# Weights on a second load queue, single first tiles and a new step list in a fused windowed-attention and MLP kernel

## The chip, the cores and the metric

The kernel runs on one core of a Trainium2 chip. The metric is the device time of one execution in microseconds (us); the median of three runs is given, and one execution was also recorded by the profiler. The core has five engines with queues of their own: PE (TensorE, matrix multiplication, with its weight loads shown as PEld), DVE (VectorE), ACT (ScalarE), POOL (GpSimd) and SP (SyncE, which here only issues transfers). DMA transfers are issued from SP's, ACT's and POOL's queues and carried out by 16 DMA engines.

## The reference

Input x is 2048 rows of 512 (bf16). All weights are bf16.

```python
xn = layernorm(x)
# A: attention over 8 keys at distances 0, 2, ... 14; 32 heads of 16
q, k, v = split(xn @ wqkv)
logits = einsum(q, k[s - 2*w]) * 16 ** -0.5      # w = 0..7, masked where s - 2*w < 0
s = (softmax(logits) @ v[s - 2*w]) @ wo
# B: a mixer and an MLP
h = gelu(layernorm(xn) @ w1)                     # 512 columns in four groups of 128
hs = concat(h0 shifted by -1, h1 by +1, h2 by -2, h3 by +2 rows) @ w2
x1 = xn + hs
g = silu(x1 + gelu(layernorm(x1) @ w3) @ w4)     # 512 -> 1376 -> 512
out = x + s * g
```

## The kernel before

The 2048 rows are cut into 4 chunks of 512, and each chunk into 4 tiles: tile i holds every fourth row of its chunk, so that 16 tiles of 128 x 512 result. Every piece of work is a small Python function, a *step*. The string `ORDER` at the top lists all steps with their arguments, `name.arg.arg`, and a loop at the end calls them in that order (lines 14 to 70 and the loop behind `so`). Each engine works off its own instructions strictly in the order in which the list has issued them; waits between engines are inserted from the data. So the list is the schedule. Nothing else decides an order.

The steps that the change and the prediction speak of, with their lines in the kernel before:

- Loads. `ldxc` (L211) loads a whole chunk of x, 512 KB; `ldxp` (L221) a pair of tiles, 256 KB; `ldv` (L234) half of v's weights, `ldw1` (L241) half of w1, each 256 KB; `ldqk` (L228) the q half or the k half of the q and k weights, 512 KB; `ldw2` (L245) 512 KB, `ldw3`, `ldw4` and `ldwo` (L270, a quarter of wo) later weights. The letter after the name is the queue: s for SP, a for ACT, g for POOL.
- Constants. `c_warm` zeroes the operand of the warm-up matmuls; `c_zero` (L288 to L290) zeroes the 14 rows ahead of v in its DRAM scratch `v_dram` by a DMA from POOL's queue, and the halo columns of `hT` by two memsets; `c_elog` (L294 to L302) and `c_sel` (L310) build selection matrices on POOL; `sqw` (L315) makes ACT load its table early; `warmup.n.w.b` (L321) runs n matmuls of width w on zeros.
- The first chunk. `st` (L333) takes the row statistics of a tile on DVE, `sq0` (L338) the root on ACT, `nm0` (L344, L345) normalises on DVE, `tr0` (L356) transposes on PE, and `ev0h` or `ev0a` (L364, L360) brings the result to `xnT` on ACT. In later chunks `nmv` (DVE, L410) or `nm` (ACT, L417) normalises, with `rp`, `rs` (POOL, L386), `rr` and `nb` for the factors, and `xT.k` (L424) transposes a pair of tiles by a DMA on SP's queue.
- Products from `xnT`. `qk.c.n` (L443, four matmuls for one eighth of q and k of a chunk; `eqk`, L452, evacuates), `v.i` (L471; `ev` L481, and `sv`, L489, stores to `v_dram` from POOL's queue), `w1.i` (L496; `eh`, L507, with Gelu; `hTr`, L515, transposes on SP's queue).
- Attention. `pw` (L530) multiplies q with shifted k on DVE, `lg` (L543) sums over a head on PE, `smx`, `ex`, `sms`, `smn` are the softmax, `tE` (L598) transposes the weights, `vl` (L710) loads v's windows, `vp` (L716) weights them on DVE, `ws` (L729) sums on PE, `eo` (L743) evacuates, `oTr` (L748) or `oTp` with `eoT` (L756, L762) transposes, `wo` (L768) and `woh` (L793, half a tile) project.
- Mixer and MLP. `w2` (L611), `xa` (L618), `st3s`, `rq`, `r3`, `nm3` (L645), `x1Tr` (L655), `w3.c.f` (L668, 44 groups of four), `eg` (L677), `w4` (L685, 16 groups of eleven), `ya` (L692), `si` (L696).
- The end. `sg` (L775), or `ge` with `gb` (L782, L786), or `sgh` (L802) multiply s with g. For tiles 0 to 11 `pre` (L828) copies x into the output beforehand and `soa` (L835) adds on the way out; for tiles 12 to 15 `fav` or `favh` adds x on DVE and `so` or `soh` (L839, L813) stores.

The PSUM holds six accumulation banks, given as the last argument of a PE step, beside the two that `lg` uses.

Of the kernel before, what the change touches and what calls it, by code (L numbers as in the profile page):

```python
# [28 lines left out]
qk.1.6.3 xa.1 nb.7 qk.1.0.2 nb.6 st3s.1 eqk.1.6 hTr.3 rr.4 xa.0 ldw3.s.0 st3s.0 eqk.1.5 pw.0.6
nm.13 nm.12 nm.15 qk.1.7.0 qk.1.3.4 w2.2.5 w1.9.3 w1.8.1 eh.9 eh.8 xa.2 rr.7 hTr.4 rr.5 rq.0  # L30
w1.10.5 pw.0.7 r3.0 v.8.3 eh.10 st3s.2 nm.14 w2.3.1 nm3.0 nm3.1 eqk.1.3 w2.5.5 ev.8 qk.2.0.4
xa.3 st3s.3 eqk.1.7 eqk.1.0 xT.6 lg.0.3 rq.1 kh.2 xa.5 lg.0.2 r3.1 w2.4.2 smx.0 ldw3.s.1 sv.8
xT.7 x1Tr.0 v.10.5 qk.2.4.0 w2.6.1 eqk.2.4 nm3.3 xa.4 ex.0 w2.7.3 w1.11.2 xa.6 st3s.6 nm3.2 xa.7
qk.2.5.1 eqk.2.0 x1Tr.1 eh.11 ev.10 sv.10 rr.6 v.9.0 v.11.3 w1.13.4 eqk.2.5 ev.9 hTr.5 qk.2.7.2
w1.15.1 eqk.2.7 w1.12.0 vl.s.2.0 vl.s.0.0 ldw4.s.2 qk.2.2.2 vl.s.3.1 eh.12 pw.1.0 st3s.4 st3s.7
st3s.5 v.12.5 eqk.2.2 pw.1.3 sms.0 eh.13 v.13.0 w3.0.6.4 ev.11 hTr.6 rq.2 qk.2.1.3 pw.1.2 r3.2
sv.9 eg.0.6 eqk.2.1 ldwo.s.3 smn.0 rq.3 pw.1.1 r3.3 w3.0.1.2 qk.2.3.4 w3.0.10.3 nm3.4 eqk.2.3
tE.0 eh.15 eg.0.10 ev.13 eg.0.1 lg.1.1 lg.1.0 pw.1.7 w2.8.1 w1.14.0 w3.0.0.2 eh.14 w3.0.2.3
hTr.7 qk.2.6.0 eqk.2.6 eg.0.0 w2.10.4 nm3.6 vl.s.0.1 nm3.7 x1Tr.3 vl.s.1.0 pw.1.5 xa.8 pw.1.4
nm3.5 pw.1.6 w2.11.1 xa.10 w3.0.8.2 xa.11 qk.3.1.4 st3s.11 eg.0.8 ev.12 w2.14.1 lg.1.2 st3s.10  # L40
sv.12 lg.1.3 eqk.3.1 w2.12.4 sv.11 st3s.8 eg.0.2 smx.1 w2.9.3 ldw4.s.1 x1Tr.2 xa.9 w2.15.5 xa.14
w3.0.3.2 w3.0.9.3 xa.12 pw.2.2 qk.3.2.1 qk.3.0.4 w2.13.0 st3s.9 eqk.3.2 eqk.3.0 eg.0.3 vl.s.9.1
ldw4.s.0 rq.4 xa.15 vl.s.9.0 vl.s.3.0 ldwo.s.2 pre.s.2 qk.3.3.1 w3.0.5.2 st3s.12 qk.3.4.5 eg.0.5
pw.2.3 eqk.3.3 qk.3.5.4 st3s.14 pw.2.4 xa.13 pw.2.1 rq.5 st3s.15 v.15.1 eqk.3.5 v.14.2 ev.15
eqk.3.4 w3.1.1.0 w3.0.4.5 vp.0 st3s.13 rq.6 pw.2.0 r3.4 nm3.9 w3.0.7.1 eg.0.4 ev.14 eg.0.9
eg.0.7 ex.1 qk.3.7.4 w3.1.0.2 eg.1.0 sv.14 r3.5 nm3.10 rq.7 nm3.11 x1Tr.5 w3.1.8.1 vl.s.2.1
pre.s.1 vl.s.10.0 vl.s.10.1 w4.1.3 eqk.3.7 ldwo.s.1 kh.3 sv.15 r3.7 c_sel sms.1 w4.0.5 w4.2.4
ya.0 smn.1 r3.6 w3.1.5.5 w4.3.2 nm3.8 ya.2 ya.1 vp.1 x1Tr.4 w3.1.9.3 nm3.15 eg.1.5 ya.3 w3.1.6.4
pre.s.0 vp.3 tE.1 w3.1.7.2 eg.1.6 eg.1.1 w3.1.3.5 w3.1.4.0 eg.1.7 vp.2 lg.2.1 lg.2.0 qk.3.6.2
eg.1.8 w3.1.10.1 eqk.3.6 nm3.14 pw.2.5 pw.2.7 w3.1.2.4 eg.1.3 eg.1.10 eg.1.4 lg.2.2 pw.2.6  # L50
x1Tr.7 eg.1.2 ws.2.1 ws.1.0 ws.0.4 eg.1.9 pw.3.2 ws.3.3 eo.1 lg.2.3 eo.0 smx.2 vl.s.4.1 w4.6.0
w3.2.0.4 oTr.0 eo.2 eo.3 oTr.1 vl.s.5.1 pw.3.0 ex.2 vl.s.4.0 vl.s.6.0 vl.s.5.0 w4.5.3 vl.s.6.1
ya.6 pw.3.4 w4.7.0 w4.4.1 w3.2.3.5 sms.2 si.2 si.1 si.3 eg.2.0 eg.2.3 si.6 vl.s.7.1 vl.s.7.0
pw.3.1 pw.3.5 nm3.12 ya.4 wo.1.4 nm3.13 ya.7 w3.2.2.1 sg.1 w3.2.9.0 vp.4 ya.5 w3.2.5.4 w3.2.4.5
eg.2.9 w3.2.1.2 smn.2 x1Tr.6 w3.2.8.0 vp.5 eg.2.4 eg.2.2 eg.2.5 w3.2.10.1 w3.2.7.4 w3.2.6.5
eg.2.7 eg.2.10 eg.2.1 eg.2.8 vp.6 tE.2 vl.s.8.1 vl.s.8.0 wo.0.3 eg.2.6 wo.2.1 wo.3.0 pw.3.3 sg.2
w4.10.5 soa.2 sv.13 sg.3 vp.7 w3.3.0.0 lg.3.0 eg.3.0 lg.3.2 si.4 pw.3.6 pw.3.7 ws.4.0 ws.5.1
lg.3.1 ws.7.2 ws.6.4 eo.4 ya.10 lg.3.3 vl.s.11.1 w4.9.0 smx.3 eo.5 si.7 si.0 eo.7 si.5 eo.6
si.10 vl.s.13.1 oTr.2 vl.s.13.0 vl.s.11.0 w4.8.2 vp.9 vl.s.12.1 ex.3 oTr.3 w4.11.4 ya.8 ya.9
sms.3 ya.11 smn.3 w3.3.7.0 w3.3.5.2 w3.3.1.5 eg.3.5 vp.10 tE.3 wo.4.4 eg.3.7 eg.3.1 vl.s.14.1  # L60
vl.s.12.0 sg.0 vl.s.14.0 vp.11 w3.3.4.1 w3.3.9.2 w3.3.10.5 eg.3.10 w3.3.8.0 w3.3.3.3 w3.3.6.5
eg.3.9 eg.3.4 vp.8 w3.3.2.1 eg.3.6 eg.3.8 wo.6.2 eg.3.2 eg.3.3 wo.7.0 sg.6 vp.13 ws.10.3 ws.9.2
eo.10 ws.11.1 ws.8.5 eo.9 w4.13.3 vl.s.15.0 sg.4 vl.s.15.1 vp.12 eo.11 eo.8 wo.5.4 si.11 oTr.5
vp.14 si.9 w4.12.5 oTr.4 w4.15.1 ya.12 sg.5 si.12 si.8 sg.7 vp.15 w4.14.0 soa.1 soa.0 soa.3
# [810 lines left out]
```

## Time and profile before

| | us |
|---|---|
| runs | 189.74, 190.42, 190.26; median 190.26 |
| profiled execution, its own time | 190.75 |
| its span, first to last instruction | 189.0 |
| PE busy / PE weight loads | 182.8 (97%) / 87.0 |
| DVE busy | 165.1 (87%) |
| ACT busy | 112.8 (60%) |
| POOL busy | 42.7 (23%) |
| chain that ended last, share of PE | 85% |
| granted TensorE clock, mean | 0.996 |

The page names an instruction by the line of the program that issued it, its engine and operation, and the tiles that it writes and reads, `out<-in`. In rows of the chain of waits a piece has its start, its length and what it was; SPq is the time that SP took to issue a transfer. In a timeline a bracket at the end gives the idle time of the engine before the piece, and what ended it. A transfer's time to landing runs from the start of its issue to the moment at which all of its data have arrived.

### The profile page before, as it was taken

How to read it: one execution, taken by the hardware profiler on the slowest of the kernel's cores; microseconds unless marked ns; L12 is line 12 of the kernel's file. 1: busy time of each engine (PE TensorE's matmuls, PEld its weight loads, DVE VectorE, ACT ScalarE, POOL GpSimd, SP SyncE). 2: the span in 40 equal slices, each digit the busy share in tenths (PEclk: the TensorE clock that was granted, in tenths of full speed). 3: DMA queues.
4: the chain of work that ended last, by engine and by line, in shares of the span. 5: the costliest groups of instructions: out<-in, count | busy, mean ns of one | idle time of the engine just before them, and what ended most of it. 6: DMA issues, size and time to landing. Idle time of an engine off the chain costs nothing.

```text
span 189.0 us, 3685 instructions
## 1 busy us (share of the span) xinstructions
PE 182.8 (97%) x1430; PEld 87.0 (46%) x1430; DVE 165.1 (87%) x270; ACT 112.8 (60%) x189; POOL 42.7 (23%) x70
## 2 busy tenths in 40 slices
...
GB/s 164 315 352 115 199 248 141 194 238 137 233 120 286 278 64 224 222 87 190 399 162 361 274 57 134 254 401 277 189 190 95 254 335 238 210 254 106 88 106 116
DMA packets 47842, 39.25 MB, mean 208 GB/s; under 512 B 35251, under 2 KB 41889, under 8 KB 47777
## 3 DMA queue, kind: packets, MB, share of 16 engines
...
q0 software_dynamic: 2528, 3.69, 10.9%
...
q10 hardware_dynamic: 288, 0.20, 0.3%
...
## 4 chain that ended last, share of the span: by engine, by line
PE 85%; DMA 4%; DVE 4%; issue 2%; POOL 2%; SPq 1%; ACT 1%; POOLq 0%
PE mm L668 20%; PE mm L685 18%; PE mm L443 15%; PE mm L611 8%; PE mm L496 7%; PE mm L471 6%; PE lg L543 4%; PE mm L768 4%; DMA xc<-in_A_x_dram 3%; PE mm L729 3%; POOL out_dram L835 2%; DMA out_dram<-xr 1%; DVE st L333 1%; DVE xr L775 1%; DVE xr L786 1%
## 5 line engine op out<-in xcount | busy, mean ns | idle before, releaser
L530 DVE TENSOR_TENSOR pw<-qT,kT 128x2048 bf16<-128x2048 bf16 x32 | 38.3, 1214 | 3.4 <-PE lg L543 2.4
L668 PE MATMUL mm<-x1T,w_sb 128*128 128x512 bf16 (+1 forms) x176 | 40.9, 379 | 0.0
L685 PE MATMUL mm<-w_sb,h 128*128 128x512 bf16 (+1 forms) x176 | 39.4, 379 | 0.0
L677 ACT ACTIVATE h<-mm 128x512 bf16<-128x512 f32 (+1 forms) x44 | 23.9, 602 | 23.3 <-PE mm L668 17.6
L716 DVE TENSOR_TENSOR vs<-vs,att 128x4096 bf16<-128x4096 bf16 x16 | 36.2, 2285 | 0.0
L443 PE MATMUL mm<-xnT,wqk_sb 128*128 128x512 bf16 x128 | 30.6, 379 | 0.0
L835 POOL DMA_DIRECT2D out_dram<-xr x12 | 11.0, 1117 | 74.0 <-DVE xr L775 74.0
L668 PEld LDWEIGHTS <-w_sb 128*128 128x128 bf16 (+1 forms) x176 | 17.6, 100 | 20.4
L685 PEld LDWEIGHTS <-h 128*128 128x128 bf16 (+1 forms) x176 | 16.9, 98 | 20.8 <-issue 0.4
L443 PEld LDWEIGHTS <-wqk_sb 128*128 128x128 bf16 x128 | 12.4, 98 | 15.0
L452 ACT ACTIVATE kT<-mm 128x512 bf16<-128x512 f32 x16 | 9.4, 601 | 12.1 <-PE mm L443 11.9
L489 POOL DMA_DIRECT2D v_dram<-vt x16 | 9.6, 601 | 30.6 <-ACT vt L481 27.2
L471 PE MATMUL mm<-w2v_sb,xnT 128*128 128x512 bf16 x64 | 15.8, 379 | 0.0
L496 PE MATMUL mm<-w_sb,xnT 128*128 128x512 bf16 x64 | 15.8, 379 | 0.0
L611 PE MATMUL mm<-w2v_sb,hT 128*128 128x512 bf16 x64 | 15.7, 380 | 0.0
L768 PE MATMUL mm<-wo_sb,oT 128*128 128x512 bf16 x60 | 14.3, 379 | 0.0
L333 DVE BATCH_NORM_STATS2 st<-xc 128x6 f32<-128x512 bf16 x16 | 10.8, 676 | 3.9 <-DMA xc<-in_A_x_dram 3.9
L452 ACT ACTIVATE qT<-mm 128x512 bf16<-128x512 f32 x16 | 9.4, 605 | 7.8 <-PE mm L443 7.7
L635 POOL TENSOR_TENSOR rstd<-nmr,mhalf 128x2 f32<-128x2 f32 x8 | 9.1, 1136 | 19.8 <-DVE nmr L628 19.7
L507 ACT ACTIVATE ht<-mm,rs 128x512 bf16<-128x512 f32 x16 | 10.6, 690 | 4.4 <-PE mm L496 2.3
L696 ACT ACTIVATE xr<-xr 128x512 bf16<-128x512 bf16 x16 | 9.6, 630 | 6.0 <-DVE xr L692 6.0
L692 DVE TENSOR_TENSOR xr<-mm,xr 128x512 bf16<-128x512 f32 x16 | 10.6, 683 | 1.1 <-PE mm L685 0.9
...
## 6 DMA issues: line engine op xcount, KB each, us to landing
...
xc<-in_A_x_dram SPq DMA_DIRECT2D x4, 256.0 KB, 5.9
...
```

The lines of the kernel that those rows point to most:

```text
L443: nc.tensor.matmul(pt, lhsT=wqk_sb[:, dt, nt * P : (nt + 1) * P], rhs=xnT[c][:, :, dt, :], start=(dt == 0), stop=(dt == ND - 1),)
L452: nc.scalar.activation(dst.rearrange("p (n i) -> p n i", i=TPC), mm.pop(("qk", c, nt)).rearrange("p (i n) -> p n i", i=TPC), AF.Copy,)
L471: nc.tensor.matmul(pt, lhsT=xnT[c][:, jj, dt, :], rhs=wv_sb[:, dt, :], start=(dt == 0), stop=(dt == ND - 1),)
L496: nc.tensor.matmul(pt, lhsT=xnT[c][:, jj, dt, :], rhs=w1_sb[:, dt, :], start=(dt == 0), stop=(dt == ND - 1),)
L530: nc.vector.tensor_tensor(out=pw_t[c, u], in0=q_t[c], in1=k_t[c][:, :, DIL * u : DIL * u + CH], op=ALU.mult)
L611: nc.tensor.matmul(pt, lhsT=hT[:, plane, g, p0 : p0 + P], rhs=w2_sb[:, g, :], start=(g == 0), stop=(g == ND - 1),)
L668: nc.tensor.matmul(pt[:fs, :], lhsT=w3_sb[:, dt, ft * P : ft * P + fs], rhs=x1T[c][:, :, dt, :], start=(dt == 0), stop=(dt == ND - 1),)
L677: nc.scalar.activation(h3[c, ft][:fs, :], mm.pop(("w3", c, ft))[:fs, :], AF.Gelu_apprx_tanh)
L685: nc.tensor.matmul(pt, lhsT=h3[c, ft][:fs, jj * P : (jj + 1) * P], rhs=w4_sb[:fs, ft, :], start=(ft == 0), stop=(ft == NF - 1),)
L716: nc.vector.tensor_tensor(out=vv, in0=vv, in1=att[c][:, :, H * jj : H * jj + H].unsqueeze(2).to_broadcast([P, NB * 2, DH, H]), op=ALU.mult,)
L768: nc.tensor.matmul(pt, lhsT=oT[i // 2][:, i % 2, dt, :], rhs=wo_sb[:, dt, :], start=(dt == 0), stop=(dt == ND - 1),)
L835: nc.gpsimd.dma_start(out=rows(out2, i), in_=xr[i], accum_op=ALU.add)
```

## The change

Four things are changed. v's weight halves go out from ACT's queue, beside x on SP's. The first pair of x tiles is loaded by two transfers of one tile each (a new step `ldx`) where there was one of two tiles. The zeroing `c_zero` stands later in the list. And the whole list of steps is new: the same computing steps on the same engines, in another order and partly with other accumulation banks (five short warm-up matmuls stand where there were eight). The unused step `fag` is taken out and an unused step `preh` is put in.

The head of the list up to the first steps of chunk 1, and its end:

```diff
-ldxp.s.0 c_warm c_small warmup.10.512.0 sqw c_ident kh.0 ldv.s.0 ldv.s.1 ldxp.s.1 ldw1.s.0
-ldw1.s.1 c_zero st.0 ldxp.s.2 ldxp.s.3 st.1 sq0.0 ldqk.s.0 ldqk.s.1 nm0.0 sq0.1 rp.0 nm0.1
-tr0.0.0 warmup.8.128.1 ev0h.0.0 ev0h.0.1 st.2 tr0.1.2 v.0.1 st.3 ev0h.1.0 ev0h.1.1 sq0.2 v.1.2
-ev.0 nm0.2 sq0.3 rp.1 w1.0.0 ev.1 nm0.3 rs.0 sv.0 st.5 tr0.2.1 ldxc.s.2 w1.1.2 ev0a.2 sv.1 rr.0
-st.4 tr0.3.3 rs.1 v.2.1 ev0a.3 st.7 rp.2 rs.2 w1.2.4 ev.2 st.6 eh.0 v.3.3 sv.2 rp.3 rr.1 w1.3.1
-nmv.4 nmv.5 ev.3 qk.0.1.5 xT.2 eh.1 sv.3 qk.0.0.3 rs.3 qk.0.3.2 eh.2 eh.3 eqk.0.1 c_elog
-qk.0.4.1 qk.0.5.5 nmv.6 nmv.7 st.11 ldxc.s.3 st.10 st.8 eqk.0.3 eqk.0.5 qk.0.2.2 eqk.0.0
-qk.0.6.4 eqk.0.2 st.9 eqk.0.4 qk.0.7.3 eqk.0.6 eqk.0.7 pw.0.1 rp.5 st.15 st.13 rp.4 xT.3 hTr.0
-ldw2.s hTr.1 w1.4.1 v.5.4 ldwo.s.0 ev.5 w1.5.3 v.4.2 ev.4 qk.1.4.4 rs.4 sv.4 v.6.5 w1.7.2 rr.3
+ldx.s.0 ldx.s.1 c_warm kh.0 ldv.a.0 warmup.10.512.0 ldv.a.1 c_small c_ident sqw st.0 st.1 sq0.0
+nm0.0 sq0.1 nm0.1 rp.0 c_elog ldxp.s.1 ldw1.s.0 ldw1.s.1 ldxp.s.2 ldqk.s.0 ldxp.s.3 st.2 st.3
+ldqk.s.1 tr0.0.1 warmup.5.128.0 ev0h.0.0 ev0h.0.1 tr0.1.2 v.0.0 ev0h.1.0 ev0h.1.1 sq0.2 v.1.1
+ev.0 sq0.3 ev.1 rs.0 nm0.2 w1.0.2 nm0.3 tr0.2.0 tr0.3.1 w1.1.3 ev0a.2 v.2.0 ldxc.s.2 ldwo.s.3
+rr.0 rp.1 sv.0 sv.1 rs.1 ev0a.3 qk.0.0.1 w1.2.4 eqk.0.0 ev.2 qk.0.3.5 st.5 st.4 rp.2 st.6 rs.2
+st.7 nmv.4 rp.3 eh.1 nmv.5 sv.2 rr.1 qk.0.4.0 st.8 xT.2 rs.3 st.9 qk.0.1.1 c_sel eh.0 nmv.6
+qk.0.7.3 eh.2 eqk.0.1 eqk.0.4 nmv.7 rp.4 ldxc.s.3 st.10 qk.0.5.2 rs.4 xT.3 st.11 qk.0.2.1
+eqk.0.5 eqk.0.7 rp.5 qk.0.6.0 hTr.0 rr.4 eqk.0.2 rs.5 eqk.0.3 v.3.3 eqk.0.6 w1.3.5 ev.3 pw.0.3
+v.4.0 eh.3 sv.3 w1.5.3 hTr.1 rr.2 ev.4 w1.4.5 sv.4 nb.4 ldw2.s c_zero qk.1.3.0 st.14 eqk.1.3
+rr.3 st.15 st.13 eh.5 qk.1.6.1 eqk.1.6 pw.0.1 st.12 nm.9 w1.7.2 eh.4 rp.7 rp.6 rs.6 qk.1.7.3
+ldw4.s.2 hTr.2 nb.5 pw.0.0 rr.5 qk.1.4.1 v.5.5 w1.6.0 eqk.1.7 eh.6 v.6.3 pw.0.2 nb.6 nm.8 rs.7
+rr.7 rr.6 w2.1.4 ev.5 ev.6 xT.4 nm.10 w2.0.0 v.7.5 vl.s.1.0 xa.0 nm.12 eqk.1.4 xa.1 lg.0.0
...
-soa.7 soa.5 soa.4 soa.6 ya.13 ya.15 si.13 ws.13.4 ya.14 ws.15.3 ws.12.1 ws.14.5 eo.15 wo.8.0
-si.14 eo.14 wo.9.3 sg.8 eo.12 eo.13 wo.10.1 soa.8 sg.9 si.15 oTp.13.4 soa.9 sg.10 oTp.14.3
-eoT.13 oTp.12.0 wo.11.5 eoT.12 oTp.15.4 eoT.14 wo.13.0 eoT.15 wo.14.3 wo.12.4 woh.15.0.1
-woh.15.1.2 soa.10 sg.11 soa.11 ge.13 gb.13 ge.14 fav.13 gb.14 so.s.13 ge.12 fav.14 gb.12 so.s.14
-sgh.15.0 fav.12 favh.15.0 so.a.12 sgh.15.1 soh.s.15.0 favh.15.1 soh.a.15.1
+sg.10 soa.7 soa.10 soa.1 ya.14 ya.13 si.14 ws.14.2 ws.13.3 ws.12.4 ya.12 ya.15 ws.15.1 wo.11.0
+eo.14 si.13 eo.13 si.11 eo.15 wo.9.3 sg.11 eo.12 oTp.14.1 soa.11 sg.9 wo.8.0 eoT.14 si.12 soa.9
+oTp.12.3 sg.8 oTp.13.1 eoT.12 wo.14.4 eoT.13 soa.8 oTp.15.3 ge.14 wo.12.0 eoT.15 gb.14 wo.13.4
+ge.12 fav.14 so.s.14 woh.15.0.3 gb.12 ge.13 woh.15.1.0 fav.12 si.15 gb.13 so.a.12 fav.13
+sgh.15.0 so.s.13 favh.15.0 sgh.15.1 soh.s.15.0 favh.15.1 soh.a.15.1
```

The steps:

```diff
     @step
+    def ldx(q, i):
+        if 0 not in x_c:
+            x_c[0] = rot("xc", 0, 2, [P, TPC, D])
+        qs[q].dma_start(out=xtile(i), in_=rows(x2, i))
+
+    @step
     def ldxc(q, c):
...
-    @step
-    def fag(i):
-        nc.gpsimd.tensor_tensor(out=xr[i], in0=xtile(i), in1=xr[i], op=ALU.add)
-
...
+    @step
+    def preh(q):
+
+        def half(t):
+            return t[(NCH - 1) * CH :, :].rearrange("(p i) d -> p (i d)", i=TPC)[:, 0 : 2 * D]
+
+        qs[q].dma_start(out=half(out2), in_=half(x2))
```

More of the change, by code (lines that the diff above doesn't have):

```diff
@@ L23 @@
-qk.0.4.1 qk.0.5.5 nmv.6 nmv.7 st.11 ldxc.s.3 st.10 st.8 eqk.0.3 eqk.0.5 qk.0.2.2 eqk.0.0
-qk.0.6.4 eqk.0.2 st.9 eqk.0.4 qk.0.7.3 eqk.0.6 eqk.0.7 pw.0.1 rp.5 st.15 st.13 rp.4 xT.3 hTr.0
-ldw2.s hTr.1 w1.4.1 v.5.4 ldwo.s.0 ev.5 w1.5.3 v.4.2 ev.4 qk.1.4.4 rs.4 sv.4 v.6.5 w1.7.2 rr.3
-rr.2 eh.4 pw.0.2 kh.1 ev.6 sv.5 rs.5 nb.4 pw.0.0 st.12 eqk.1.4 eh.5 w1.6.1 qk.1.1.4 qk.1.2.3
-v.7.5 hTr.2 nm.8 nm.9 w2.1.0 pw.0.3 nb.5 rp.6 eh.6 xT.4 vl.s.1.1 eh.7 st.14 rp.7 lg.0.0 rs.7
-eqk.1.2 lg.0.1 ev.7 pw.0.5 w2.0.5 rs.6 eqk.1.1 nm.11 nm.10 pw.0.4 sv.7 qk.1.5.4 sv.6 xT.5
@@ L29 @@
[L29 to L64, printed above, removed]
@@ new lines @@
+eqk.0.5 eqk.0.7 rp.5 qk.0.6.0 hTr.0 rr.4 eqk.0.2 rs.5 eqk.0.3 v.3.3 eqk.0.6 w1.3.5 ev.3 pw.0.3
[3 more added lines that the diff above has]
+rr.7 rr.6 w2.1.4 ev.5 ev.6 xT.4 nm.10 w2.0.0 v.7.5 vl.s.1.0 xa.0 nm.12 eqk.1.4 xa.1 lg.0.0
+lg.0.1 eh.7 st3s.1 w2.3.4 qk.1.5.2 qk.1.1.1 nm.11 hTr.3 ev.7 nm.13 pw.0.4 xT.5 w2.2.5 eqk.1.5
@@ new lines @@
+sv.5 kh.1 sv.7 w1.8.2 st3s.0 pw.0.6 ldw3.s.0 eh.8 pw.0.7 v.8.0 xa.3 qk.1.2.3 nb.7 pw.0.5 nm.14
+qk.1.0.4 w1.9.2 eqk.1.1 xT.6 eqk.1.0 v.9.1 eh.9 st3s.3 rq.0 eqk.1.2 hTr.4 ev.8 lg.0.3 lg.0.2
+xa.2 st3s.2 rq.1 nm.15 w1.10.3 smx.0 xT.7 qk.2.7.0 eh.10 qk.2.6.2 w1.11.3 eqk.2.6 v.10.5 kh.2
+sv.6 r3.1 sv.8 r3.0 nm3.3 nm3.2 ev.9 x1Tr.1 sv.9 w2.5.1 ev.10 eh.11 v.11.2 xa.5 eqk.2.7 hTr.5
+nm3.1 pw.1.2 pw.1.3 nm3.0 w2.6.3 ev.11 w1.13.0 ldw3.s.1 w1.12.2 eh.13 x1Tr.0 eh.12 xa.6 st3s.5
+ex.0 v.12.1 ldw4.s.0 hTr.6 qk.2.3.0 w1.15.3 qk.2.2.2 w2.7.5 pw.1.0 pw.1.1 ev.12 w1.14.1 eh.15
@@ new lines @@
+st3s.6 w2.8.4 xa.7 eh.14 st3s.7 qk.2.0.3 vl.s.3.1 vl.s.1.1 hTr.7 v.14.1 w2.4.5 eqk.2.3 eqk.2.0
+sv.11 vl.s.0.0 ldw4.s.1 ldwo.s.0 eqk.2.2 lg.1.1 lg.1.0 vl.s.0.1 w3.0.6.2 sms.0 xa.4 rq.3 r3.3
+st3s.4 pw.1.5 w2.9.5 eg.0.6 w3.0.3.3 rq.2 xa.9 r3.2 sv.10 pw.1.6 w3.0.0.2 eg.0.3 ev.14 sv.14
+w2.10.5 qk.2.4.1 eqk.2.4 eg.0.0 nm3.4 nm3.6 nm3.7 pw.1.4 nm3.5 w2.11.3 qk.2.5.0 x1Tr.3 eqk.2.5
+xa.8 smn.0 x1Tr.2 qk.2.1.2 w3.0.8.4 eg.0.8 pw.1.7 w3.0.7.0 qk.3.5.1 eqk.2.1 vl.s.2.1 tE.0
+w3.0.2.2 eqk.3.5 w3.0.9.4 st3s.9 xa.11 st3s.11 st3s.8 eg.0.9 eg.0.2 lg.1.3 lg.1.2 vl.s.2.0
```

23 lines of the change are left out of this document (added).

## The prediction

> **What bounds the kernel now.** I read the page's busy table first (PE 182.8 of 189.0 us), then the chain of waits in order of time, then stretches with the busy time of each engine, and last the DMA view cut down to single issues.
>
> The stretches (us, then busy us and instructions of PE, PEld, DVE, ACT, POOL; clock; DMA share; GB/s):
>
> ```profile
> 16.00:170.00 154.00, 153.98 (x1255) 73.36 (x1254) 142.97 (x214) 94.38 (x155) 29.29 (x44) 1.00 0.90 216
> 170.00:184.60 14.60, 14.55 (x107) 7.07 (x104) 10.57 (x16) 8.85 (x16) 6.99 (x8) 1.00 0.76 102
> ```
>
> From 16 to 184.6 us PE idles for 0.07 us in all. Both step lists hold the same computing steps (three warm-up matmuls aside; fag and preh are in neither), so nothing can be gained there: the new list can only start this dense stretch earlier, end it faster, or tear holes into it. What holds its start back is the chain of the first 16 us (start, length, what):
>
> ```profile
> 0.73 0.40 SPq L221
> ...
> 2.15 5.68 DMA xc<-in_A_x_dram
> ...
> 7.85 0.71 DVE st L333
> ...
> 9.64 0.42 DVE xr L345
> ...
> 10.11 0.40 PE mm L356 x4
> 10.51 0.94 PE mm L496 x4
> ```
>
> The second pair of x tiles (I call it p1) is issued at 2.15, behind x0 and both halves of v's weights on SP's queue, and lands at 7.83; statistics and normalisation take 2.28 us more, and tr0.2 starts at 10.11. PE in that time:
>
> ```profile
> 5.87 0.61 PE L356 MATMUL mm<-ident,xr 128*128 128x128 bf16 x4 [0.24 <-DVE xr L345]
> ...
> 7.06 1.94 PE L471 MATMUL mm<-w2v_sb,xnT 128*128 128x512 bf16 x8
> 8.83 1.03 PE L496 MATMUL mm<-w_sb,xnT 128*128 128x512 bf16 x4
> 10.11 0.40 PE L356 MATMUL mm<-ident,xr 128*128 128x128 bf16 x4 [0.26 <-DVE xr L345]
> ```
>
> A group of four matmuls costs 0.8635 us where PE is dense (32 of qk in 6.91). v.0, v.1 and w1.0 (2.59) run from 7.06 to about 9.70, then PE waits. The DMA view, one issue each in order of issue (KB, us from issue to landing):
>
> ```profile
> xc<-in_A_x_dram SPq DMA_DIRECT2D x1, 256.0 KB, 2.9
> w2v_sb<-in_A_wqkv_dram SPq DMA_DIRECT2D x1, 256.0 KB, 3.1
> w2v_sb<-in_A_wqkv_dram SPq DMA_DIRECT2D x1, 256.0 KB, 5.5
> xc<-in_A_x_dram SPq DMA_DIRECT2D x1, 256.0 KB, 5.7
> w_sb<-in_B_w_dram SPq DMA_DIRECT2D x1, 256.0 KB, 5.8
> w_sb<-in_B_w_dram SPq DMA_DIRECT2D x1, 256.0 KB, 6.0
> ```
>
> Added to their issue times in SP's timeline (0.73, 1.18, 1.64, 2.15, 2.66, 3.14) this is a ladder: 0.25 MB in at 3.6, 0.50 at 4.3, 0.75 at 7.17, 1.0 at 7.83, 1.25 at 8.5, 1.5 at 9.18; the next rows go on with 2.0 at 10.5, 2.5 at 12.0, 3.0 at 13.3. v's second half lands 0.3 us before the third matmul of v.0 needs it. In 2 to 7 us the DMA share is 0.79, 0.88, 0.78, 0.74 and 0.83, so 0.98 us of engine time lie idle there.
>
> **The change, part by part.** *Start.* SP now issues x0 and x1 (128 KB each), p1, w1's halves, pair 2, q's half of wqk, pair 3, k's half. ACT issues v's halves at about 0.73 and 1.1.
> - p1 is issued at 0.73 + 2 × 0.45 = 1.6 instead of 2.15, with only 0.5 MB through its own ring. How the two rings share is not in this trace. Bounds: if v waits, p1 completes 0.50 MB (4.3); if v goes first, 1.0 MB (7.83). Middle 0.75 MB: 7.17.
> - v's second half completes 0.75 MB if v goes first (7.17), 1.5 MB if x and w1 go first (9.18). Middle 1.125 MB: 8.17.
> - Two rings can fill the idle 0.98 us; bounds 0 and 0.98. I take three quarters, 0.73, since the zeroing DMA of POOL (issued 1.50, 0.73 us) leaves this stretch too. So p1 at 6.4, v at 7.45, w1's second half at 8.45.
>
> x0 alone (half the bytes of the pair) should be in by about 3.0 to 3.6, and the ten warm-up matmuls end at 5.63 either way, so tr0.0 moves from 5.87 to 5.63 and v.0 from 7.06 to about 6.7 (five short warm-ups instead of eight, 0.08 each). Then: v.0's third matmul waits for 7.45; v.0 ends at 7.88, v.1 at 8.74, w1.0 at 9.61 (its third matmul needs w1 by 9.18). tr0.2 is ready at 6.4 + 2.28 = 8.7 and costs no wait; two transposes at 0.22 reach 10.05. Five groups (w1.1, v.2, w1.2, v.3, w1.3, in whatever order among qk) end in effect at 10.05 + 4.32 = 14.37. Before, that point was 15.13. **Gain 0.76 us.** At 7.17 it would be 1.04, at 8.17 only 0.04.
>
> By the Trainium skill, "DMA: Bandwidth & Descriptors", section "Issuing engines are not separate DMA queues", queues of different engines feed the same 16 DMA engines and a second issuer saves only issue time. By that rule v's second half comes earlier by 0.4 us of issue alone, 8.17 - 0.4 = 7.77, and the gain would be 0.44; the idle DMA share above speaks for some more.
>
> *ACT.* The two issues (0.37 each by ACT's rows at the end) push the table load (1.28) and the first Sqrt (0.20) from 2.22 to about 2.96; the first real Sqrt comes at 4.56 now and not before 3.8 then. Nothing, with 0.8 us of cover; beyond that it would cost its excess on x0's chain.
>
> *POOL.* The zeroing (DMA issue 0.73, two memsets of 0.35; it zeroes v_dram's pad rows and hT's halo) moves behind sv.4, where POOL idles 6.01 us in front of 25.89; its first readers on PE are w2.1 and w2.0 at about 31. The constants e_log (2.35 us, now at 17.52) go into POOL's idle time before 5.98. Both nothing.
>
> *SP.* ldwo.3 (0.74) now stands ahead of xT.2, and pair 3 behind q's half of wqk, so pair 3 lands at the 2.5 MB step, 12.0 - 0.7 = 11.3 instead of 10.5. DVE reaches st.6 at about 11.6, so it hides. q's half lands at the 2.25 MB step, 11.2; qk.0.0, now right after v.2, wants it at 10.05 + 1.73 = 11.78.
>
> *The list after 16 us.* I added up each engine's steps with spacings from the rows (pw 1.13, vp 2.20, xa, ya and sg 0.61, smx 2.4; lg 0.58, ws 0.46, w4 2.38 on PE). PE work ahead of the first ws of each chunk, minus DVE work up to that chunk's last vp: before 10.2, 9.2, 10.5, 10.9; after 10.6, 10.5, 10.2, 12.3. For the first w3 against the last nm3: before 12.2, 22.7, 23.7, 21.3; after 14.6, 21.2, 36.3, 30.5. The cover is no thinner, so I cost the reordering at nothing between 16 and 184 us. If that is wrong, each us that a producer is late costs a us, since PE has no idle time to absorb it.
>
> *Tail.* After the last ge (0.60) DVE still has gb, fav, two sgh and two favh before the last store, as now (184.34 to 186.29). si.15 (0.53) moves behind the last ge on ACT and is done 0.2 us before sgh.15.0. Nothing.
>
> **Sum.** The profiled execution took 190.75 (span 189.0 and 1.75 around it); it would become 189.99 with a span of 188.24. The median of the runs is 0.49 lower, 190.26: forecast **189.50**. The unknown terms alone give -1.1 (PE runs without a wait from 6.7: 6.7 + 2.59 + 0.44 + 4.32 = 14.05) to about 0: 189.1 to 190.3.
>
> **Rivals.** *A: hidden anyway.* The 16 groups between tr0.3 and qk.1.3 end at 10.05 + 13.82 = 23.87. qk.1.3 needs the transpose xT.3, now issued at 18.89 behind a 512 KB x load, 5.6 us to landing, at 24.49. If it lands no earlier than now, PE waits 0.62 and 0.14 of the gain is left: 190.1. For it: it hangs on pair 3, which comes later. Against: the wait of 2.45 us for POOL's rs that delays it now should shrink, and I get 17.5 for its issue.
>
> *B: the other side, v's weights late.* Place: the third matmul of v.0. If SP's ring, filled first and longer, is served ahead of ACT's, v's second half comes with 1.5 MB, at 9.18. Then v.0 ends at 9.61, w1.0 at 11.34, and the point at 15.13 becomes 16.10: 191.2. It decides from 8.2 on (no gain); each later us costs a us. For it: v.0 is only 0.3 us from waiting now. Against: ACT's issues are as early as SP's. The Trainium skill, "DMA: Bandwidth & Descriptors", section "Queues, rings and completion order", says that each DMA engine takes turns between its queue rows packet by packet; by that rule B would not happen. No run here shows two hardware rings at the start.
>
> *C: a hole later in the list.* w2's weights (4.2 us to landing now) are issued behind hTr.1, which needs w1.3, done at 10.05 + 13 × 0.8635 = 21.3 instead of 15.1. With the evacuation (0.69) and hTr.1's own issue (1.34) they go out at 23.4, and w2.1 wants them at 23.87 + 8 × 0.8635 = 30.8. At the slowest 512 KB row (8.2) they come at 31.6: 0.8 us. Two such holes make 0.76 - 1.6 a loss of 0.84: 191.1.
>
> **How the numbers follow.** Within 0.5% (0.95 us, about what a measurement of this kernel can tell from no change) means 189.31 to 191.21. Forecast 0.62, of which 0.28 lies below 189.31 (v by about 7.2) and 0.34 within. A 0.12, all within. B 0.15 and C 0.11, of which a wait somewhat past the price worked out, 0.24, goes beyond 191.21 and 0.02 stays within; the share beyond is large because a late transfer has no upper bound in these rows. Faster 0.28, same 0.48, slower 0.24. The forecast's own range is 189.1 to 190.2; with half of B and C outside and 0.3 for the spread of the runs the range is 188.8 to 191.4.
>
> **What would show it.** Right: p1 at 6.4 ± 0.5, v.0's third matmul at 7.2 to 7.8, the first of tr0.2 before 9.8, PE without idle time from there to about 183.8, zeroing at 23 to 26 on POOL with nobody waiting. Wrong: a PE gap at v.0 past 8.2 (B), at qk.1.3 (A), at w2.1 (C), or any PE idle time over 0.3 us between 16 and 184.

## The result, and the profile after

| | before | after |
|---|---|---|
| median of 22 runs | 189.88 (189.74 to 190.50) | 190.41 (190.26 to 192.31) |
| ratio, 95% interval | | 1.003 (1.0019 to 1.0041) |
| profiled execution / its span | 190.75 / 189.0 | 190.69 / 188.9 |

The changed kernel is 0.5 us slower, not 0.8 faster. The two profiled executions hide it, as they took the same time; that of before was 0.87 over its kernel's median. So a second one of before, from the first experiment (189.95, span 188.2, called "before again" below), is set beside that of after. The median of 22 runs of before is also 0.38 below that of the three runs from which the forecast was counted (190.26).

The stretches of after (start:end, length, busy us and instructions of PE, PEld, DVE, ACT, POOL; clock; DMA share; GB/s):

```profile
16.00:170.00 154.00, 153.06 (x1241) 73.31 (x1253) 141.08 (x211) 94.37 (x155) 24.87 (x38) 1.00 0.85 214
170.00:184.60 14.60, 14.23 (x104) 6.96 (x103) 10.60 (x17) 8.69 (x16) 7.37 (x9) 1.00 0.82 121
```

PE is nearly as dense as before. Of the 0.94 us of idle time up to 170, twelve are single steps of 0.05, 0.63 in all, which I put down to missing records of matmuls (14 fewer than in before's stretch); two are waits, of 0.16 and 0.15. The chain of after's start (start, length, what):

```profile
0.74 0.39 SPq L212
...
1.19 3.55 DMA xc<-in_A_x_dram
...
4.76 0.70 DVE st L339
...
5.67 0.06 DVE rs L350
...
5.75 0.42 DVE xr L351
...
6.22 0.40 PE mm L362 x4
```

The chain runs over the second single tile, x1: issued at 1.19, in at 4.74. VectorE has the statistics of x1 (L339) in front of the normalization of x0 (L350, L351), so x0, in at 3.65, helps nothing. The transfers of after, one issue each in order of issue (KB, us to landing; issued at 0.74, 0.74, 1.19, 1.25 and 1.65):

```profile
w2v_sb<-in_A_wqkv_dram ACTq DMA_DIRECT2D x1, 256.0 KB, 3.6
xc<-in_A_x_dram SPq DMA_DIRECT2D x1, 128.0 KB, 2.9
xc<-in_A_x_dram SPq DMA_DIRECT2D x1, 128.0 KB, 3.5
w2v_sb<-in_A_wqkv_dram ACTq DMA_DIRECT2D x1, 256.0 KB, 4.2
xc<-in_A_x_dram SPq DMA_DIRECT2D x1, 256.0 KB, 4.5
```

PE of after, at the start and at the one later wait that a rival had named:

```profile
6.22 0.40 PE L362 MATMUL mm<-ident,xr 128*128 128x128 bf16 x4 [0.59 <-DVE xr L351]
...
7.10 1.90 PE L477 MATMUL mm<-w2v_sb,xnT 128*128 128x512 bf16 x8
...
9.70 0.61 PE L362 MATMUL mm<-ident,xr 128*128 128x128 bf16 x8
...
24.28 1.04 PE L449 MATMUL mm<-xnT,wqk_sb 128*128 128x512 bf16 x4 [0.16 <-DMA xnT<-xr]
```

tr0.2 starts at 9.70 without a wait, as forecast. But before again has that too. Its chain, and the landing of its p1 (issued at 2.15):

```profile
0.73 2.63 DMA xc<-in_A_x_dram
...
5.78 0.50 PE mm L356 x4
...
9.58 0.22 PE mm L356 x4
...
14.34 6.91 PE mm L443 x32
```

```profile
xc<-in_A_x_dram SPq DMA_DIRECT2D x1, 256.0 KB, 4.1
```

Its x pair is in at 3.36, its first transposes start at 5.78, p1 is in at 6.20, and from 5.78 on PE has no idle time over 0.03. The last line is the point that the prediction puts at 15.13 in the profile of before and forecasts at 14.37:

```profile
15.13 6.91 PE mm L443 x32
```

Before again has it at 14.34 without any change. Of these 0.79 us, 0.42 are the wait for p1 (w1.0 to tr0.2 takes 10.11 - 8.83 there, 9.41 - 8.55 here), 0.28 a later v.0 (7.06 and 6.78), and 0.09 lie behind tr0.2. Between the first transposes and PE's last product the two kernels need the same (184.29 - 6.22 = 178.07 and 183.76 - 5.78 = 177.98). VectorE's last steps, before again first, then after:

```profile
183.55 0.43 DVE L786 TENSOR_TENSOR xr<-vt,xr 128x512 bf16<-128x512 bf16 x1
183.90 0.42 DVE L802 TENSOR_TENSOR xr<-mm,xr 128x256 bf16<-128x256 f32 x1
184.23 0.41 DVE L819 TENSOR_TENSOR xr<-xc,xr 128x512 bf16<-128x512 bf16 x1
...
185.22 0.29 DVE L807 TENSOR_TENSOR xr<-xc,xr 128x256 bf16<-128x256 bf16 x1
```

```profile
184.07 0.42 DVE L792 TENSOR_TENSOR xr<-vt,xr 128x512 bf16<-128x512 bf16 x1
184.53 0.43 DVE L825 TENSOR_TENSOR xr<-xc,xr 128x512 bf16<-128x512 bf16 x1
184.88 0.42 DVE L808 TENSOR_TENSOR xr<-mm,xr 128x256 bf16<-128x256 f32 x1
...
185.99 0.29 DVE L813 TENSOR_TENSOR xr<-xc,xr 128x256 bf16<-128x256 bf16 x1
```

VectorE ends 1.75 behind PE's last product before (185.51 - 183.76), 1.99 after (186.28 - 184.29). So 0.44 is lost at the first transposes, 0.09 in between and 0.24 at the end: 0.77, against 0.74 between the two executions' times.

### The profile page after: what moved, and what is told of

It is laid out like the page before. It is cut to its first block, busy times and chain, and to the rows that moved or that the text cites. A ratio compares the mean times of both kernels' runs of the same rounds, so it can differ in the third digit from the quotient of the medians.

```text
span 188.9 us, 3664 instructions
## 1 busy us (share of the span) xinstructions
PE 181.5 (96%) x1412; PEld 86.6 (46%) x1427; DVE 164.7 (87%) x270; ACT 112.0 (59%) x188; POOL 40.6 (21%) x70
## 3 DMA queue, kind: packets, MB, share of 16 engines
HBM read 26.41 MB, written 5.78 MB: 170 GB/s over the span
## 4 chain that ended last, share of the span: by engine, by line
PE 85%; DMA 6%; DVE 3%; ACT 2%; issue 1%; POOL 1%; SPq 0%
PE mm L674 20%; PE mm L691 20%; PE mm L449 12%; PE mm L617 7%; PE mm L477 6%; PE mm L502 5%; PE mm L774 5%; PE lg L549 4%; PE mm L735 4%; DMA xnT<-xr 4%; DMA xc<-in_A_x_dram 2%; ACT oT L768 1%; PE mm L362 1%; POOL rs L392 1%; ACT vt L788 0%
## 5 line engine op out<-in xcount | busy, mean ns | idle before, releaser
L674 PEld LDWEIGHTS <-w_sb 128*128 128x128 bf16 (+1 forms) x176 | 17.5, 100 | 20.1
L641 POOL TENSOR_TENSOR rstd<-nmr,mhalf 128x2 f32<-128x2 f32 x8 | 6.5, 818 | 38.0 <-DVE nmr L634 38.0
L339 DVE BATCH_NORM_STATS2 st<-xc 128x6 f32<-128x512 bf16 x16 | 10.8, 677 | 2.7 <-DMA xc<-in_A_x_dram 2.7
L749 ACT ACTIVATE o<-mm 128x512 bf16<-128x512 f32 x16 | 8.9, 594 | 7.2 <-issue 4.7
```

What stands on the lines that cost most here:

```text
L339: nc.vector.bn_stats(out=st1[:, i, :], in_=xtile(i))
L674: nc.tensor.matmul(pt[:fs, :], lhsT=w3_sb[:, dt, ft * P : ft * P + fs], rhs=x1T[c][:, :, dt, :], start=(dt == 0), stop=(dt == ND - 1),)
```

## The experiments

Eighteen runs. Times are medians; a ratio is to before, run on the same chip. Diffs show the tokens of the step list that differ, with a few beside them.

**Was the wait for the second x pair usual, and which part of the change costs?** e1 is the kernel before, unchanged.

> The kernel before, unchanged, profiled a second time. Theory (the profiled execution before was one with a late DMA engine at its start; a usual execution has none): the second pair of x tiles lands at 6.2 to 6.9 instead of 7.83, tr0.2 starts before 9.5, the span is 188.0 to 188.3. Rival (the start of the profiled execution is the usual one, the new list or the new loads cost later): pair at 7.5 to 8.0 and span 188.8 to 189.2 again.

189.94, ratio 0.9993 (0.9982 to 1.0004). In its profile p1 was in at 6.20, not 7.83, and tr0.2 followed without a wait. The two later profiles of the old list with its loads (e11 and e18) have p1 in at 6.86 and 6.92 and no such wait either, so of four the profile of before alone has it. Over ten profiles with all loads on SP's queue, the last of the 16 DMA engines finishes p1 0.57 to 1.88 behind the median engine; the profile of before is the 1.88. e2 is the old list with the new loads (the kernel before first, then e2):

```diff
-ldxp.s.0 c_warm c_small warmup.10.512.0 sqw c_ident kh.0 ldv.s.0 ldv.s.1 ldxp.s.1 ldw1.s.0
+ldx.s.0 ldx.s.1 c_warm c_small ldv.a.0 ldv.a.1 warmup.10.512.0 sqw c_ident kh.0 ldxp.s.1 ldw1.s.0
```

> The list before, with the new first loads alone (x0 and x1 apart, v's halves from ACT's queue). Theory: x1 lands at about 4.7 instead of 3.6 and delays tr0.0 by 0.3, nothing is gained by the pair behind it, 0.0 to 0.4 us slower than before. Rival 1 (the loads gain what was forecast, the list loses it): 0.4 to 0.8 us faster. Rival 2 (the loads alone make the whole loss): 0.5 us slower.

190.39, ratio 1.0044 (1.0017 to 1.007): the loads alone make a loss as large as the whole. x1 was in at 4.84:

```profile
6.33 0.40 PE L362 MATMUL mm<-ident,xr 128*128 128x128 bf16 x4 [0.70 <-DVE xr L351]
```

The first transposes start 0.55 later than in e1, and the profiled time is 0.46 longer. e3 is the new list with the old loads, e4 the new list with v on ScalarE's queue but the first pair in one load:

```diff
-ldx.s.0 ldx.s.1 c_warm kh.0 ldv.a.0 warmup.10.512.0 ldv.a.1 c_small c_ident sqw
+ldxp.s.0 ldv.s.0 ldv.s.1 c_warm kh.0 warmup.10.512.0 c_small c_ident sqw
...
+ldxp.s.0 c_warm kh.0 ldv.a.0 warmup.10.512.0 ldv.a.1 c_small c_ident sqw
```

> The new list with the first loads as before (x0 and x1 in one load, then both halves of v, all on SP's queue). Theory: tr0.0 at 5.9, and of the 0.5 us loss 0.2 to 0.4 stay (wait for xT.3, tail). Rival 1 (list loses, loads gain): 1 us slower than before. Rival 2 (loads alone lose): as before within 0.1.

> The new list with x0 and x1 in one load again, v's halves still on ACT's queue. Theory: the pair lands by 4.2, before x1 alone did (4.74), tr0.0 starts at 5.9 or earlier, 0.2 to 0.4 us faster than the changed kernel. Rival (splitting the pair is not what makes x1 late, v beside it is): pair at 4.6 to 4.8, no gain.

e3: 190.61, scattered from 189.93 to 191.62, ratio 1.0034 (1.0013 to 1.0054). e4: 190.30, ratio 1.0013 (1.0003 to 1.0024); the pair in at 3.90 instead of 3.36 and the transposes at 6.18. So v beside x makes x late in either form, and the list has a cost of its own. The two do not add up: against before on the same chip (189.98) the loads alone cost 0.41, the list alone 0.63, and both together 0.53 in the run of the result. e5 is the kernel before and has the split alone, with v behind it on SP's queue:

```diff
-ldxp.s.0 c_warm c_small warmup.10.512.0 sqw c_ident kh.0 ldv.s.0
+ldx.s.0 ldx.s.1 c_warm c_small warmup.10.512.0 sqw c_ident kh.0 ldv.s.0
```

> The old list and the old queues; only the first x pair is split into two loads of one tile each on SP's queue, with v's two loads behind them on SP's queue. Theory 1 (what delays the second x tile is v's bytes, which the second queue lets in beside x): x1 has only x0 ahead of it, lands at 3.4 to 3.9, the first transposes start at 5.6 to 5.8 as with the pair, v half a microsecond later than with the pair without harm, time 189.8 to 190.0, ratio 0.999 to 1.001. Rival (a load of one tile has a fixed cost of its own, so that the split alone delays the second tile): x1 lands at 4.2 or later, the transposes at 6.1 or later, 190.2 to 190.4, ratio 1.001 to 1.003.

190.16 (189.46 to 190.68), ratio 1.0002 (0.9987 to 1.0017). x1 was in at 3.62: the split is not what made it late, v on the second queue is (e2 has the same split). The gain at the first transposes and its loss behind (PE of e5):

```profile
5.46 0.40 PE L362 MATMUL mm<-ident,xr 128*128 128x128 bf16 x4 [0.53 <-DVE xr L351]
...
8.94 0.59 PE L502 MATMUL mm<-w_sb,xnT 128*128 128x512 bf16 x2 [0.21 <-DMA w_sb<-in_B_w_dram]
```

The transposes start at 5.46 instead of 5.78, but that needed more than an early x: the ten warm-ups ended at 4.94 in this execution, where they end at 5.63 in before again.

**Why does the new list scatter with the old loads?** VectorE in e3:

```profile
14.96 0.69 DVE L339 BATCH_NORM_STATS2 st<-xc 128x6 f32<-128x512 bf16 x1 [1.07 <-DMA xc<-in_A_x_dram]
```

The new list has the statistics of tiles 8 and 9 in front of the normalizations of 6 and 7, on which xT.3 and then qk.1.3 hang; the old list has them behind. This profile is of one of e3's faster executions (190.21), PE has no idle time in it from 7 to 170, and no slow one was profiled; that the slow ones hang on xT.3 is a supposition. Both kernels that try it start from e3: e6 issues xT.3 before the last x load, e7 turns VectorE's order round:

```diff
-nmv.7 rp.4 ldxc.s.3 st.10 qk.0.5.2 rs.4 xT.3 st.11
+nmv.7 rp.4 st.10 qk.0.5.2 rs.4 xT.3 ldxc.s.3 st.11
...
-qk.0.4.0 st.8 xT.2 rs.3 st.9 qk.0.1.1 c_sel eh.0 nmv.6 qk.0.7.3 eh.2 eqk.0.1 eqk.0.4 nmv.7 rp.4
+qk.0.4.0 xT.2 rs.3 qk.0.1.1 c_sel eh.0 nmv.6 qk.0.7.3 eh.2 eqk.0.1 eqk.0.4 nmv.7 st.8 st.9 rp.4
```

> The new list with the old loads, as in the run before of that kind (190.61, 189.93 to 191.62); only the fourth transpose (xT.3) is issued on SP before the load of the last x chunk. Theory 2 (the scatter comes from qk.1.3, which has no slack for xT.3, and xT.3 shares the DMA engines with that load): xT.3 lands by 22, the slower executions vanish, all within 189.9 to 190.4, median 190.1, what is left being the tail. Rival (the scatter arises elsewhere, in a later load): the spread stays 189.9 to 191.6 with a median of 190.4 to 190.7.

> The new list with the old loads; only VectorE's order is changed: the two normalizations of tiles 6 and 7 come before the statistics of tiles 8 and 9, as in the old list. Theory 2a (slow executions are those in which the third x chunk lands late, VectorE waits for it at the statistics of tile 8, and the normalizations, xT.3 and qk.1.3 behind wait too): the slower executions vanish, highest at most 190.5, median 190.0 to 190.2. Theory 2b (xT.3 is late because of the load ahead of it on the queue, not because VectorE was late): spread and median stay as they were, 190.4 to 190.7 and up to 191.6.

e6: 190.14 (189.88 to 190.97), ratio 1.0019 (1.0004 to 1.0034); e7: 190.11 (189.93 to 190.83), ratio 1.0008 (0.9996 to 1.0019). The medians fell by 0.5, and the five executions over 191.1 are gone, though neither stayed below the highest time expected, and the intervals of both ratios overlap that of e3: likely, not shown. From issue to landing xT.3 took 7.0 in after and 3.9 in e6:

```profile
xnT<-xr SPq DMA_TRANSPOSE x1, 7.0
```

```profile
xnT<-xr SPq DMA_TRANSPOSE x1, 3.9
```

**The tail.** e8 and e9 are the changed kernel with VectorE's last steps interleaved:

```diff
-gb.12 ge.13 woh.15.1.0 fav.12 si.15 gb.13 so.a.12 fav.13 sgh.15.0 so.s.13 favh.15.0
+gb.12 ge.13 woh.15.1.0 si.15 gb.13 fav.12 so.a.12 sgh.15.0 fav.13 favh.15.0 so.s.13
...
+gb.12 ge.13 woh.15.1.0 fav.12 si.15 gb.13 so.a.12 sgh.15.0 fav.13 favh.15.0 so.s.13
```

> The changed kernel as it is, but VectorE's last steps take turns between the tiles as in the old list, so that no step follows at once on the one whose result it reads. Theory 3 (dependent pairs on VectorE cost 0.45 a step against 0.34, 0.26 in the tail, and go straight into the end): 190.1, 0.2 to 0.3 below the 190.4 of the changed kernel, ratio to before 1.000 to 1.001. Rival (the end is set by ScalarE's release of the last gate values or by the last stores, not by VectorE's spacing): 190.3 to 190.45, ratio 1.002 to 1.003.

> The changed kernel, with VectorE's last steps in the old list's order this time: the add of tile 12 stays ahead of the gate of tile 13 and fills the time until ScalarE has released it, and the half step of tile 15 stands between the gate and the add of tile 13. In the earlier run on the tail VectorE waited 0.44 at 184.03 for ScalarE, which the moved add no longer filled. Theory 3' (spacing costs, once that wait is filled): VectorE ends 1.75 behind TensorE as in the old list instead of 2.0 to 2.1, time 190.1 to 190.2, ratio to before 1.001. Rival (ScalarE's release sets the end whatever the order): 190.35 to 190.55, ratio 1.002 to 1.004.

Neither helped: 190.52, ratio 1.0044 (1.0022 to 1.0065), and 190.56, ratio 1.0045 (1.002 to 1.0069). In e9 the half step of tile 15 comes at 184.61, where ScalarE's silu of tile 15 ends (183.96 + 0.62 = 184.58):

```profile
183.96 0.62 ACT L702 ACTIVATE xr<-xr 128x512 bf16<-128x512 bf16 x1
```

So VectorE's order alone was not the cause; ScalarE has four silus to do after 175.5 where the old list has two. e16 moves that one forward and lets VectorE multiply tile 14's gate from the product itself (sg for ge and gb); VectorE's order is that of e9, so against e9 only ScalarE's share changes:

```diff
-soa.8 oTp.15.3 ge.14 wo.12.0 eoT.15 gb.14 wo.13.4
+soa.8 oTp.15.3 si.15 wo.12.0 eoT.15 sg.14 wo.13.4
...
-gb.12 ge.13 woh.15.1.0 fav.12 si.15 gb.13 so.a.12 fav.13 sgh.15.0 so.s.13 favh.15.0
+gb.12 ge.13 woh.15.1.0 fav.12 gb.13 so.a.12 sgh.15.0 fav.13 favh.15.0 so.s.13
```

> The changed kernel with a third tail: silu of tile 15 two steps earlier on ScalarE, and tile 14's gate multiplied by VectorE straight from the product (0.69 in its idle 1.25) instead of a ScalarE copy of 0.60 and a multiplication of 0.42; VectorE's order as in the second tail. Theory 3'' (ScalarE is full from 176 on, its silu of tile 15 releases the half step of tile 15 at 184.6): VectorE ends 1.75 behind TensorE, 190.1 to 190.25 where the changed kernel has 190.41. Rival (the end is set by the last stores or by something else behind VectorE): VectorE ends earlier but the time stays at 190.35 to 190.55.

VectorE ends 1.74 behind PE (187.68 - 185.94). The median, 190.30, stands 0.27 over that of before on its chip (190.03), where the changed kernel stood 0.53 over on its own; the ratio over all runs is 1.003 (1.0008 to 1.0051), for two of twelve took 192.1.

**The other parts.** e10 is e3 with the repairs of e6, e7 and e9 together; e12 is e10 with e5's split; e11 is the kernel before with c_zero moved:

```diff
-ldw1.s.1 c_zero st.0
+ldw1.s.1 st.0
...
-ldw2.s hTr.1 w1.4.1
+ldw2.s c_zero hTr.1 w1.4.1
```

> The new list with the old loads and three repairs together: normalizations of tiles 6 and 7 ahead of the statistics of tiles 8 and 9, xT.3 issued before the last x load, and the tail of the run before. Theory (these three places are all that the new list costs): median 189.8 to 190.0, ratio 0.999 to 1.001, highest about 190.8, as the old list has. Rival (the list costs something elsewhere too): median 190.1 or more, ratio 1.001 to 1.003.

> The kernel before, with the zeroed rows and the two memsets of GpSimd moved behind the load of w2's weights, as the new list has them; nothing else. Theory (the prediction's step: this move costs and gains nothing, as GpSimd waits 2.3 for ScalarE anyway and 14 KB are little beside 2.5 MB): 189.9, 189.75 to 190.8 as before, ratio 0.999 to 1.001. Rival (its store is what makes one DMA engine late in some executions): the executions of 190.2 to 190.8 vanish, median 189.8, highest at most 190.1. Other rival (it meets xT.3 or w2's weights at 24): 190.2 or more.

> As the repaired list, but with the first x pair split into two loads on SP's queue and v behind them on the same queue (the change's first part without its second). Theory 1 (a split with nothing beside it gains what the earlier x0 gives, 0.2 to 0.3 at the first transposes, as in the run of the split on the old list, 189.46 at best): fastest executions 189.4 to 189.6, median 189.6 to 189.8, ratio 0.998 to 0.9995. Rival (the later weights behind the additional load take it back, as the wait of 0.21 at 8.73 in that run shows): 189.9 to 190.2, ratio 1.000 to 1.001.

e10: 190.34 (189.81 to 191.19), ratio 1.0017 (1.0002 to 1.0032): the list is not repaired by these three, as the tail is not. e11: 190.30, ratio 1.0009 (0.9992 to 1.0026): no effect that these runs can tell, though the median lies 0.30 over before's, where the last rival put it; and DMA engines were late without the zeroing too (p1 at 6.86). e12: 190.69 (190.09 to 191.88), ratio 1.0036 (1.002 to 1.0052): the split did not pay here; PE waited at 8.2, 8.9, 9.6 and 10.3 for weights and p1, which was in at 7.61. What makes a DMA engine late stays open.

**v on ScalarE's queue, but later.** e13 (changed kernel) and e14 (old list) have both ldv.a steps behind sqw; e15 has v's first half on SP's queue and the second behind sqw. The diff shows e14 and then e15 against e2; e13's list is changed like e14's:

```diff
-ldx.s.0 ldx.s.1 c_warm c_small ldv.a.0 ldv.a.1 warmup.10.512.0 sqw c_ident
+ldx.s.0 ldx.s.1 c_warm c_small warmup.10.512.0 sqw ldv.a.0 ldv.a.1 c_ident
...
+ldx.s.0 ldx.s.1 ldv.s.0 c_warm c_small warmup.10.512.0 sqw ldv.a.1 c_ident
```

> The changed kernel, with v's two loads still on ScalarE's queue but issued behind its table load and first activation, at about 2.25 and 2.75 instead of 0.74 and 1.25. Theory 1' (the loss at the start is v's bytes beside x's second tile): x1 lands at 3.5 to 3.8 instead of 4.74, the first transposes start at 5.4 to 5.7 instead of 6.22, v lands at 6.0 to 6.6; 189.9 to 190.15, the tail's part being left. Rival (v is then late itself: the first product with v waits): v's second half at 6.9 or later, TensorE idle 0.4 or more before that product, 190.2 to 190.5.

> The old list with the change's loads (two single x tiles on SP, v on ScalarE) and v issued behind ScalarE's table load. Theory 1' with a steadier queue (two queues: no packet that stalls over 0.5): 189.4 to 189.6, highest 189.9, ratio 0.997 to 0.9985, below both kernels. Theory 1' without it: 189.5 to 190.7 as in the run of the split on SP's queue. Rival (v late): 189.9 to 190.3.

> As the run before, but v's first half on SP's queue right behind x's two tiles, and only the second half on ScalarE's queue behind the table load. If v was late in the run before, it is not here: both halves in by 6.2, 189.4 to 189.6. If v was in time there, this is the same or 0.1 slower, since the second x pair is one load later (in by 5.6 instead of 5.0). A packet that stalls over 0.5 in the profile would say that two queues do not prevent it.

None did what it was made for: ScalarE issued v at 0.86 to 0.96, while its table load (0.72 to 2.00) was still running. x1 came at 4.89, 4.90 and 4.95, and the times were 191.33 (7 runs), 190.38 and 190.53, ratios 1.0086 (1.0053 to 1.0118), 1.0037 (1.0012 to 1.0061) and 1.0041 (1.0017 to 1.0066). e15 adds that one half of v beside x is as bad as two. v issued truly later was not tried.

**Executions of 192.** Of the 112 executions of the changed kernel, e2, e4, e8, e9 and e13 to e16, 20 took over 191.9; of 180 of the kernel before, none. In the profiles of these kernels PE is idle for 0.59 to 1.15 between the warm-ups and the first transposes, in before for 0.24. Where this gap is 0.59 or 0.65 (after and e4), 1 of 33 executions was long; where it is 0.66 to 1.15 (the others), 19 of 79. One of the 20 was profiled, in e16 (192.08). Its PE:

```profile
6.43 0.61 PE L362 MATMUL mm<-ident,xr 128*128 128x128 bf16 x4 [0.79 <-DVE xr L351]
...
7.79 2.96 PE L477 MATMUL mm<-w2v_sb,xnT 128*128 128x512 bf16 x8
```

The eight products of v take 2.96 instead of 1.90: up to about 10 us each takes 0.43, the pace of the warm-ups, where the others take 0.22. The view by stretches gives a granted clock of 1.00 from 4 to 12 us in both kernels, but it counts the time ahead of the trace's first clock record as full speed. The records themselves begin, at full clock, at 9.95 in this execution and at 5.79 in after, and at 9.95 the distance between two products falls from 0.43 to 0.22. e17 narrows the gap behind the warm-ups in the changed kernel, e18 opens one in the kernel before:

```diff
-warmup.10.512.0
+warmup.11.512.0
...
+warmup.8.512.0
```

> The changed kernel with 11 warm-up products of 512 columns instead of 10, nothing else: the gap of 0.59 in front of the first transposes shrinks to 0.1 to 0.2. Theory (the gap decides whether TensorE's fast pace is there when the first products come; the median's loss comes from x's late second tile): no execution above 191.5, median unchanged at 190.3 to 190.5. Rival (the slow executions come from elsewhere, a late transfer for instance): one in six still at 192 or more, so about 2 of 12. Other rival (the gap itself cost the median): median 190.0 or less.

> The kernel before with 8 warm-up products of 512 columns instead of 10, nothing else: they end 0.86 earlier, so a gap of about 1.0 in front of the first transposes, which start at 5.8 as before. Theory: most executions as before at 189.8 to 190.4, but some, two or more of 12, at 191.4 to 192, 1.6 to 1.9 above, which the kernel before has had in none. Rival (the slow executions belong to the second queue or the new loads): none above 191.

e17: the gap is 0.32 in its profile; 190.49, highest 191.00, ratio 1.0023 (1.001 to 1.0036). None of the eleven is long, but the changed kernel had one long one in 22, so this run alone says little of them. The median is still 0.30 over before's (190.19), as x1 is still late (4.90): a smaller gap does not win the loss back. e18: two groups, 189.83 to 189.93 (five) and 191.34 to 192.01 (six), one of 190.49 between, ratio 1.0032 (1.0005 to 1.0058). PE of e18, in an execution of 191.40:

```profile
5.79 0.61 PE L356 MATMUL mm<-ident,xr 128*128 128x128 bf16 x4 [1.02 <-DVE xr L345]
...
7.47 2.68 PE L471 MATMUL mm<-w2v_sb,xnT 128*128 128x512 bf16 x8
```

Here the clock records begin at 9.07; in the eighteen profiles other than this and e16's they begin between 4.10 and 6.92. So in these two executions TensorE stayed at half pace until 9 or 10 us, behind a gap of 0.79 (e16) and 1.02 (e18). That the other long ones are of this kind is likely but was not profiled. e18 also has two warm-ups fewer; the long ones behind all ten warm-ups (19 of 79) speak for the gap alone. No version beat the kernel before.

## Why the prediction was wrong

- **The step that failed first: "x0 alone (half the bytes of the pair) should be in by about 3.0 to 3.6 ... so tr0.0 moves from 5.87 to 5.63".** x0 came at 3.65, but the first transposes hang on x1, as VectorE's list has st.1 in front of nm0.0, and x1 came at 4.74 since v's halves shared the DMA engines with it (3.62 in e5, with v behind it). tr0.0 started at 6.22, 0.44 later than in before again. I weighed how the two rings share for p1 and for v, and not for x itself, which stands ahead of everything. With even sharing, x and the first half of v come together as 0.50 MB, which the prediction's ladder has in at 4.3: an estimate of x1 that stood ready. Neither list has nm0.0 in front of st.1; that was not tried.
- **"Before, that point was 15.13. Gain 0.76 us."** was taken from an execution with a wait for p1 and a late v.0, and before again has the point at 14.34, below the forecast 14.37. p1 at 6.18, tr0.2 at 9.70 without a wait and v.0's third product at 7.54 all came as I wrote they would, and nothing was gained. I set a gain read from an execution of 190.75 against a median 0.49 lower; the 0.49 was the sign that this execution had losses of its own.
- **"The list after 16 us ... nothing"**: half right. PE stayed dense, but qk.1.3 has no slack for xT.3. Rival A had the place and the transfer; it cost 0.16 in this profile, not 0.62. I had its issue at 17.5 (it was 17.19); with the 5.6 us of before it would have been in time, but it took 7.0. Both times it stands behind an x load, so the load alone does not explain the difference, and what does stays open. With the old loads, e6 and e7 took 0.5 off the median.
- **"Tail. ... si.15 ... is done 0.2 us before sgh.15.0. Nothing."** 0.24. In after's own order si.15 (ended at 184.56) comes before sgh.15.0 (184.88), but it bars any better order (e9); the missing piece was ScalarE's load in the last 8 us, which I had not added up. e16 takes ge.14 off ScalarE and moves si.15 forward, and VectorE ends 1.74 behind PE instead of 1.99.
- **POOL and ScalarE's start**: costless, as forecast; the zeroing came at 23.91 and nobody waited for it.
- **Rival B** did not happen: v was early (4.36 and 5.46), and x paid for it. By the Trainium skill, "DMA: Bandwidth & Descriptors", section "Queues, rings and completion order", the engines take turns between rings; x1's landing of 4.74 beside v and 3.62 without it (e5) agrees. I had used that rule to free v, and not to burden x.
- **Rival C** did not happen: no wait for w2's weights.
- **Not foreseen at all**: that the gap in front of the first transposes can cost 1.4 to 2.1 us in some executions. The Trainium skill, "TensorE: Matmul & The Clock Gate", part 1, "The HAM clock gate", says that TensorE runs at half rate until it has been busy through a window of about 3.4 us, and that these windows run free of the kernel's start. The pace of 0.43 against 0.22, and its coming in some executions alone, agree. So do the clock records: the stretch at full clock lasts 180.91 or 184.32 in all twenty profiles, 53 and 54 times 3.413. How much idle time a window may hold is not shown.
